# Tile-by-tile waits behind a closed pool, and three more steps at the entry of an interleaved attention

## The chip, the cores and the metric

The kernel runs on one core of one Trainium2 chip. Five engines work side by side, each through its own row of instructions in a fixed order, and wait for one another by semaphores: TensorE (PE in the profile), VectorE (DVE), ScalarE (ACT), GpSimd (POOL) and SyncE (SP), which issues most of the transfers (DMAs). The metric is the device time of one execution in microseconds (us).

## The reference, cut to what matters

Three stages follow one another: a masked attention over 4 batches, 8 heads, 576 positions and 64 columns; a dense layer that multiplies two projections; and a mixture of 8 experts of which each token uses the best two.

```python
scores = scale * np.matmul(q, k.transpose(0, 1, 3, 2))
mask_local = (rel >= 0) & (rel < 32)                       # heads 0 to 3
mask_strided = (rel >= 0) & (pos[None, :] % 32 == pos[:, None] % 32)   # heads 4 to 7
attn = softmax(np.where(masks, scores, -1e9))
x = (attn @ v).transpose(0, 2, 1, 3).reshape(2304, 512)

x = ((x @ w_a) * (x @ w_b)) @ w_out                        # 512 -> 1536 -> 512

noisy = x @ w_gate + np.log1p(np.exp(x @ w_noise)) * noise
top2 = np.argpartition(-noisy, 2, axis=1)[:, :2]           # weights: softmax of the two
out[mask] += top2_w * (np.maximum(x[mask] @ w1[e], 0.0) @ w2[e])
```

`w_a`, `w_b` and `w_out` arrive as 64-bit numbers.

## The kernel before, in words

**Arithmetic.** A product of 32-bit matrices is done as three matmuls on a high and a low part of each operand (`mm3`, L196 to L198). The weights of the dense layer are read as 64-bit words (`load_raw`, L168; tiles named `raw`) and taken apart on ACT (L178, L179, L182) and DVE (L177, L181, L184 to L186): that is "the conversion" of a block, done in two steps of a generator `conv`. A `raw` tile is one of three that are used in turn, so a load waits for the conversion three blocks earlier.

**Start.** A pool `setup` holds helper tiles from which DVE and POOL build the masks (L78 to L111; the last one is L90 on DVE). It is closed, and the pools `ring`, `stage` and `router` (L147 to L149) take over its memory. The first loads of q, k and v go into tiles of `ring` (named `qkv`, L229 to L244). Meanwhile PE runs 14 matmuls on ones (L75), which only occupy it.

**Attention.** A `Unit` is a pair of heads of one batch. Its work is cut into small methods: `T` transposes q and k (L258; copies L260, L262), `Q` computes scores of one half (L281, L290) and, after its second call, the softmax (`E`: L294, L296, L314 to L327 on DVE, L300, L318, L323 on ACT), `P` transposes probabilities (L335, copy L336), `PV` multiplies by v (L348, copy L351). `att_pipe` strings them into steps; each `yield` ends a step. For each unit the steps are Q(0,0), Q(0,1), then P(1,0) and P(1,1) of the unit before, Q(1,0), PV(1) of the unit before, Q(1,1), two T of the next unit, P(0,0), P(0,1), two T, PV(0). For the first unit of a pipe there is no unit before, and the three steps P, P and PV are left out altogether. A finished unit's tail columns go out by a store into `tails` (L353), issued by SP.

**Two pipes.** The four units of batch 0 run first, alone, with the first 12 conversion steps dealt out over their steps (`conv_to(min(12, i * 12 // 50))`, `i` counts the steps); PE's order there is the scheduler's, by its own model of the times. The twelve units of batches 1 to 3 are a second pipe, interleaved with the dense layer. This layer goes over five chunks of columns (`c`) and twelve blocks (`f`): `stage_a` computes `pa` and `pb` (12 matmuls each) and multiplies them (L703, L708 to L710), `stage_b` adds to `po` (12 matmuls). After each of these groups `point()` advances the second pipe by up to two steps. Here PE's order is the program's; DVE's and ACT's are the scheduler's. At the last block of a chunk, attention steps that the next chunk needs are run off in one go.

**Routing.** After a chunk, `finish` and `route` choose experts and write a table by eight indirect stores from POOL (L510) out of a tile `pay`, of which there are two. Its columns of token numbers are copied by DVE (L501); the scheduler places that copy early, for a `pay` that is used later, so it waits until the stores out of the tile two chunks earlier have landed. Then come the experts (`ph`, `py`), which the change does not touch.

**Small PSUM tiles.** All `tt` tiles (transposes, scores, PV of the second pipe) share two banks: a PE instruction that writes one waits until ACT or DVE has copied out the one before the last.

Of the kernel before, what the change touches and what calls it, by code (L numbers as in the profile page):

```python
# [32 lines left out]
def attention_moe_kernel(ctx: ExitStack, tc: tile.TileContext, q, k, v, w_a, w_b, w_out,  # L33
# [110 lines left out]
            yield  # L144


    ring = ctx.enter_context(tc.tile_pool(name="ring", bufs=1))  # L147
    stage = ctx.enter_context(tc.tile_pool(name="stage", bufs=1))
    rpool = ctx.enter_context(tc.tile_pool(name="router", bufs=1))  # L149

    def load_unit(src, hi, lo):

# [204 lines left out]
    def att_pipe(us, ahead, done, may=lambda u: True):  # L357

        for i in range(4):
            us[0].T(i)
            yield
        if ahead < len(us):
            us[ahead].load_qk()
        for n, u in enumerate(us):
            last = us[n - 1] if n else None
            nxt = us[n + 1] if n + 1 < len(us) else None
            for x in range(2):
                u.Q(0, x)  # L370
                yield
            if last:
                for x in range(2):
                    last.P(1, x)
                    yield
            u.Q(1, 0)
            yield
            if last:
                last.PV(1)
                done(last)  # L380
                if ahead == 1:
                    u.load_v()
                yield
            u.Q(1, 1)
            yield
            for i in range(2):
                if nxt:
                    nxt.T(i)
                    yield
            for x in range(2):  # L390
                u.P(0, x)
                yield
            for i in range(2, 4):
                if nxt:
                    nxt.T(i)
                    yield
            if nxt and n + 1 + ahead < len(us):
                us[n + 1 + ahead].load_qk()
            while not may(u):
                yield  # L400
            u.PV(0)
            yield
        for x in range(2):
            u.P(1, x)
            yield
        u.PV(1)
        done(u)
        yield
# [262 lines left out]
    with tc.manual_schedule(engines={mybir.EngineType.SP}):  # L671
        for i, u in enumerate(us):
            u.load_qk()
            u.load_v()
            conv_room["ahead"](min(i + 1, 3))
        later = [Unit(atile, bank1, b, hp, "act" if b == 1 else "dve", (b > 1,) * 2) for b in range(1, B) for hp in HPS]
        later[0].load_qk()
        later[0].load_v()
        for i, _ in enumerate(att_pipe(us, 9, lambda u: split_kd(0, u.hp))):
            conv_to(min(12, i * 12 // 50))  # L680
        conv_to(12)
        late_load()
# [4 lines left out]
    attended = set()  # L687
    may = [1]
    attq.append(att_pipe(us, 1, lambda u: attended.add((u.b, u.hp)), lambda u: u.b <= may[0]))

    def stage_a(c, f, point):
# [331 lines left out]
```

## Time and profile before

| | us |
|---|---|
| median of 3 runs | 1148.36 |
| their lowest and highest | 1148.26, 1151.85 |
| the profiled execution, its device time | 1152.77 |
| its span (first to last instruction) | 1150.9 |
| busy: PE | 1104.0 |
| busy: DVE, ACT, POOL | 511.5, 433.3, 142.8 |
| mean granted TensorE clock (1 is full speed) | 0.955 |

PE is counted busy for 96% of the span. So a gain must come from the few stretches where PE stands, or where its clock is granted at half. In the 40 slices of the page (28.8 us each) both lie at the front: the clock digits are 6, 5, 5 and 8 in the first four slices, and 9 (full) in nearly all others. Rows of the timeline give start and duration of an instruction, and in brackets how long its engine stood idle before it and what ended that.

### The profile page before, as it was taken

The numbers are of one execution on the slowest core, as the hardware profiler recorded it, in microseconds if no ns is written. First come the engines' busy times: TensorE is split into PE (matmuls) and PEld (weight loads), VectorE is DVE, ScalarE is ACT, GpSimd is POOL, SyncE is SP. The second block draws the span as 40 slices with busy tenths as digits, with TensorE's granted clock in tenths as the row PEclk, the third lists the DMA queues.
The fourth block names the chain that finished last, engine by engine and source line by source line (L and its number), as shares of the span: only waits on it lengthen the run. The fifth ranks groups of instructions, "written<-read, shape, count | busy, mean of one in ns | idle before, by whom it ended". The sixth has DMA issues, their size and how long they took to land.

```text
span 1150.9 us, 16118 instructions
## 1 busy us (share of the span) xinstructions
PE 1104.0 (96%) x6411; PEld 934.6 (81%) x6411; DVE 511.5 (44%) x1075; ACT 433.3 (38%) x935; POOL 142.8 (12%) x136
## 2 busy tenths in 40 slices
PE   7988999999999999999997999999999999999996
PEld 4756777787787877888887989998999899998995
DVE  4839787845446354223125452255343434342211
ACT  4757877533233232212124442244242323332110
POOL 0000000001000020002000314231021312121112
PEclk6558999999999999999999999999999999999998
DMA  8444443310112111730003443176344544442123
GB/s 168 112 132 135 141 146 105 78 59 12 36 36 63 39 17 49 267 118 1 1 37 94 132 142 55 42 176 178 111 113 126 121 117 118 120 111 47 19 29 48
DMA packets 88549, 105.02 MB, mean 91 GB/s; under 512 B 43664, under 2 KB 48400, under 8 KB 88464
## 3 DMA queue, kind: packets, MB, share of 16 engines
q1 hardware_dynamic: 78352, 82.89, 24.4%
q0 software_dynamic: 10112, 21.02, 10.0%
q8 instruction: 52, 0.85, 0.3%
q14 instruction: 33, 0.27, 0.1%
HBM read 78.53 MB, written 25.35 MB: 90 GB/s over the span
## 4 chain that ended last, share of the span: by engine, by line
PE 81%; DMA 6%; DVE 4%; ACT 4%; issue 2%; POOL 1%; SPq 1%; ACTq 0%; DVEq 0%; POOLq 0%
PE ph L197 6%; PE ph L196 6%; PE ph L198 6%; PE py L196 6%; PE py L197 6%; PE py L198 6%; PE po L196 4%; PE pa L196 4%; PE pb L196 4%; PE po L198 4%; PE po L197 4%; PE pb L197 4%; PE pb L198 4%; PE pa L197 4%; PE pa L198 4%; PE tt L290 2%
## 5 line engine op out<-in xcount | busy, mean ns | idle before, releaser
L873 DVE SCALAR_TENSOR_TENSOR hl<-ph,hh 128x256 fp32r<-128x256 f32 (+1 forms) x128 | 62.4, 489 | 214.4 <-ACT hh L872 213.8
L872 ACT ACTIVATE hh<-ph 128x256 fp32r<-128x256 f32 (+1 forms) x128 | 55.1, 433 | 226.3 <-PE ph L198 222.2
L708 DVE TENSOR_TENSOR a<-a,pb 128x512 f32<-128x512 f32 (+1 forms) x60 | 37.9, 631 | 128.2 <-PE pb L198 128.1
L897 POOL DMA_INDIRECT out_dram<-y,tb x40 | 64.5, 1612 | 185.3 <-ACT y L896 144.0
L510 POOL DMA_INDIRECT table<-pay,sli x36 | 35.8, 994 | 412.8 <-DVE sli L498 321.6
L703 ACT ACTIVATE a<-pa 128x512 f32<-128x512 f32 (+1 forms) x60 | 33.1, 551 | 127.6 <-PE pa L198 127.5
L709 ACT ACTIVATE gh<-a 128x512 fp32r<-128x512 f32 (+1 forms) x60 | 35.1, 586 | 79.2 <-DVE a L708 78.9
L763 POOL DMA_INDIRECT g<-x,tb x40 | 40.0, 1000 | 188.1 <-PE tt L772 166.1
L710 DVE TENSOR_TENSOR gl<-a,gh 128x512 fp32r<-128x512 f32 (+1 forms) x60 | 38.0, 634 | 17.7 <-ACT gh L709 17.3
L335 PE MATMUL tt<-ident,s 72*72 72x72 f32 (+1 forms) x224 | 30.7, 269 | 10.1 <-DVE sst L326 4.4
L290 PEld LDWEIGHTS tt<-kT,qT 64*72 64x72 f32 (+1 forms) x336 | 29.6, 149 | 11.9 <-issue 9.8
L335 PEld LDWEIGHTS tt<-ident,s 72*72 72x72 f32 (+1 forms) x224 | 23.2, 144 | 18.8 <-ACT a L703 4.8
L290 PE MATMUL tt<-kT,qT 64*72 64x72 f32 (+1 forms) x336 | 37.7, 254 | 0.0
L336 ACT ACTIVATE pT<-tt 128x288 f32<-128x288 f32 (+1 forms) x64 | 25.2, 407 | 30.9 <-PE tt L335 30.8
L196 PE MATMUL py<-w6h,hh 128*128 128x512 f32 x80 | 31.9, 401 | 2.8 <-ACT hh L872 2.8
L196 PE MATMUL pa<-xh,w0h 128*128 128x512 f32 (+1 forms) x80 | 32.7, 409 | 1.5 <-ACT xh L414 1.4
L196 PE MATMUL pb<-xh,w1h 128*128 128x512 f32 (+1 forms) x80 | 32.7, 409 | 0.0
L196 PE MATMUL py<-w2h,hh 128*128 128x512 f32 x80 | 31.9, 401 | 0.0
L196 PE MATMUL py<-w3h,hh 128*128 128x512 f32 x80 | 31.8, 398 | 0.0
L197 PE MATMUL py<-w6l,hh 128*128 128x512 f32 x80 | 31.8, 397 | 0.0
L196 PE MATMUL pa<-xh,w3h 128*128 128x512 f32 (+1 forms) x80 | 31.7, 396 | 0.0
L197 PE MATMUL py<-w3l,hh 128*128 128x512 f32 x80 | 31.6, 395 | 0.0
(294 smaller groups left out, 3294.9 us busy)
## 6 DMA issues: line engine op xcount, KB each, us to landing
st<-in_moe_w_dram SPq DMA_DIRECT2D x64, 512.0 KB
out_dram<-zero SPq DMA_DIRECT2D x13, 512.0 KB
raw<-in_moe_w_a_dram SPq DMA_DIRECT2D x4, 1024.0 KB
raw<-in_moe_w_b_dram SPq DMA_DIRECT2D x4, 1024.0 KB
raw<-in_moe_w_out_dram SPq DMA_DIRECT2D x4, 1024.0 KB
x<-row SPq DMA_DIRECT2D x16, 256.0 KB
raw<-in_moe_w_a_dram SPq DMA_DIRECT2D x4, 512.0 KB
raw<-in_moe_w_b_dram SPq DMA_DIRECT2D x4, 512.0 KB
```

Source lines behind the costliest of these rows:

```text
L196: nc.tensor.matmul(ps, w[0], x[0], start=start, stop=False)
L197: nc.tensor.matmul(ps, w[0], x[1], start=False, stop=False)
L198: nc.tensor.matmul(ps, w[1], x[0], start=False, stop=stop)
L290: nc.tensor.matmul(ps[:, ii, :], self.qT[r0:r0 + 64, q0:q0 + n], self.kT[r0:r0 + 64, k0:k0 + m], start=not pemask, stop=not pemask or ii = ...
L335: nc.tensor.transpose(ps[:, ii, :], self.s[half][:, x, ii, :], ident[:n, :n])
L510: ins = nc.gpsimd.indirect_dma_start(out=table, out_offset=bass.IndirectOffsetOnAxis(ap=sli[:, 2 * j + kk:2 * j + kk + 1], axis=0), in_=pa ...
L708: nc.vector.tensor_mul(a, a, pb)
L710: behind[0] = nc.vector.tensor_sub(gl, a, gh.bitcast(F32))
L763: nc.gpsimd.indirect_dma_start(out=g, out_offset=None, in_=x2, in_offset=bass.IndirectOffsetOnAxis(ap=TB[e, t][:, 0:1], axis=0))
L872: nc.scalar.activation(hh, ph, AF.Relu)
L873: nc.vector.scalar_tensor_tensor(hl, ph, 0.0, hh.bitcast(F32), op0=OP.max, op1=OP.subtract)
L897: ins = nc.gpsimd.indirect_dma_start(out=out, out_offset=bass.IndirectOffsetOnAxis(ap=TB[e, t][:, 0:1], axis=0), in_=y, in_offset=None, co ...
```

## The change

Three pools get `reuse_waits="tile"`: where such a pool takes memory that an earlier pool has given back, each of its tiles waits for the earlier tiles that it overlaps, and no longer for the whole earlier pool. And in `att_pipe` the three steps of the unit before are now yielded also where there is no unit before: they are empty steps of the first unit of a pipe, three for each of the two pipes.

```diff
-    ring = ctx.enter_context(tc.tile_pool(name="ring", bufs=1))
-    stage = ctx.enter_context(tc.tile_pool(name="stage", bufs=1))
-    rpool = ctx.enter_context(tc.tile_pool(name="router", bufs=1))
+    ring = ctx.enter_context(tc.tile_pool(name="ring", bufs=1, reuse_waits="tile"))
+    stage = ctx.enter_context(tc.tile_pool(name="stage", bufs=1, reuse_waits="tile"))
+    rpool = ctx.enter_context(tc.tile_pool(name="router", bufs=1, reuse_waits="tile"))
...
-            if last:
-                for x in range(2):
+            for x in range(2):
+                if last:
                     last.P(1, x)
-                    yield
+                yield
             u.Q(1, 0)
             yield
             if last:
...
                 if ahead == 1:
                     u.load_v()
-                yield
+            yield
             u.Q(1, 1)
```

The engines' rows change in many places, since the schedule is made anew, up to the second chunk of the dense layer; from there on they are almost the same.

The first place is SP's row at the start of the program, with the semaphores that an instruction waits for. Before:

```order
L229 DMA qkv_177<-in_q_dram 96x6x64 [waits DVE_49,Pool_49]
L229 DMA qkv_177<-in_q_dram 96x6x64
L229 DMA qkv_177<-in_k_dram 96x6x64 x2
L237 DMA qkv_182<-in_v_dram 128x2x64
L240 DMA qkv_182<-in_v_dram 128x5x64 x2
L168 DMA raw<-in_moe_w_a_dram 128x4x256
```

Now:

```order
L229 DMA qkv_177<-in_q_dram 96x6x64 x2
L229 DMA qkv_177<-in_k_dram 96x6x64 x2
L237 DMA qkv_182<-in_v_dram 128x2x64
L240 DMA qkv_182<-in_v_dram 128x5x64 x2
L168 DMA raw<-in_moe_w_a_dram 128x4x256
```

The first load, and with it all that stands behind it, no longer waits for DVE and POOL.

The second place is DVE's row where the second pipe starts inside the dense layer. `s_885` and `sst_886` are scores and sums of the first half of its first unit; those of the second half are `s_928` and `sst_929` before, `s_944` and `sst_945` now; `raw_861` is the first weight block of the following pair of `f`. Before:

```order
L314 TENSOR_REDUCE sst_929<-s_928 96x6
L185 TENSOR_SCALAR raw_663<-ct_265 128x1024
L710 TENSOR_TENSOR gl_924<-a_859,gh_923 128x512
L321 TENSOR_SCALAR sst_929<-sst_929 96x6
L181 SCALAR_TENSOR_TENSOR ct_265<-raw_796,ct_265 128x1024
L186 SCALAR_TENSOR_TENSOR w1l_157<-raw_663 128x4x256
L185 TENSOR_SCALAR raw_796<-ct_265 128x1024
L325 TENSOR_SCALAR sst_886<-sst_886 96x6
L186 SCALAR_TENSOR_TENSOR w2l_159<-raw_796 128x1024
L326 RECIPROCAL sst_886<-sst_886 96x6
L325 TENSOR_SCALAR sst_929<-sst_929 96x6
L327 TENSOR_TENSOR s_885<-s_885,sst_886 96x768
```

Now:

```order
L185 TENSOR_SCALAR raw_633<-ct_265 128x1024
L710 TENSOR_TENSOR gl_924<-a_859,gh_923 128x512
L186 SCALAR_TENSOR_TENSOR w1l_157<-raw_633 128x4x256
L181 SCALAR_TENSOR_TENSOR ct_265<-raw_796,ct_265 128x1024
L325 TENSOR_SCALAR sst_886<-sst_886 96x6
L177 TENSOR_SCALAR ct_265<-raw_861 128x1024
L185 TENSOR_SCALAR raw_796<-ct_265 128x1024
L326 RECIPROCAL sst_886<-sst_886 96x6
L314 TENSOR_REDUCE sst_945<-s_944 96x6
L186 SCALAR_TENSOR_TENSOR w2l_159<-raw_796 128x1024
L327 TENSOR_TENSOR s_885<-s_885,sst_886 96x768
```

The second half's sums no longer stand ahead of the first half's last step L327, but its reduction L314 still does, and the first conversion of `raw_861` (L177) has moved in ahead of it. On PE, four groups of 12 matmuls instead of three now lie between the scores of the first half and its transposes L335, which wait for L327.

The third place is DVE's row in the second chunk, at the early copy into `pay`. Before:

```order
L302 TENSOR_TENSOR s_2696<-tt_2730,maskAB_72 96x384
L314 TENSOR_REDUCE sst_2697<-s_2696 96x6
L501 COPY pay_4728<-ids_80 128x4 x2
L317 TENSOR_TENSOR s_2696<-s_2696,sst_2697 96x768
L319 TENSOR_REDUCE sst_2697<-s_2696 96x6
```

Now:

```order
L302 TENSOR_TENSOR s_2696<-tt_2730,maskAB_72 96x384
L314 TENSOR_REDUCE sst_2697<-s_2696 96x6
L317 TENSOR_TENSOR s_2696<-s_2696,sst_2697 96x768
L501 COPY pay_4728<-ids_80 128x4 x2
L319 TENSOR_REDUCE sst_2697<-s_2696 96x6
```

The subtraction L317, for which ACT's exponentials (L318) wait, has moved from behind the copy to ahead of it.

## Rows read from the trace of the kernel before

**Rows 1.** Page: granted clock in 40 slices of 28.8 us, in tenths.

```profile
PEclk6558999999999999999999999999999999999998
```

**Rows 2.** Windows: length, busy (x count) per engine, clock, DMA share, GB/s.

```profile
25.00:30.00 5.00, 5.00 (x42) 3.60 (x40) 3.97 (x8) 4.29 (x11) 0.00 (x0) 0.50 0.99 253
```

**Rows 3.** Waits of SP in 0 to 6 us: total, times, longest.

```profile
SPq L229 <- DVE maskAB L90: 4.4, 1, 4.4
```

**Rows 4.** Timeline of all engines, 0 to 45 us: start, duration, instruction, idle before.

```profile
1.07 6.01 PE L75 MATMUL idle<-ones 128*128 128x512 bf16 x14 [1.07 <-DVE ones L77]
...
5.21 1.41 SPq L229 DMA_DIRECT2D qkv<-in_q_dram  x2
...
9.30 0.69 PE L258 MATMUL sc<-ident,qkv 96*128 96x96 f32 x6 [2.22 <-DMA qkv<-in_q_dram]
...
22.05 0.65 ACT L179 ACTIVATE raw<-raw 128x512 uint32<-128x512 uint32 x1 [2.93 <-DMA raw<-in_moe_w_b_dram]
```

**Rows 5.** Timeline of ACT, 60 to 125 us.

```profile
72.73 1.10 ACT L179 ACTIVATE raw<-raw 128x1024 uint32<-128x1024 uint32 x1 [2.45 <-DMA raw<-in_moe_w_out_dram]
```

**Rows 6.** Chain of work that ended last, 55 to 80 us: start, duration, what.

```profile
55.82 5.19 DMA raw<-in_moe_w_a_dram
...
66.14 0.34 SPq L353
...
66.58 6.08 DMA raw<-in_moe_w_out_dram
...
76.61 0.80 PE pa L196
```

**Rows 7.** Timeline of DVE, 40 to 140 us, the end of batch 0.

```profile
56.36 0.69 DVE L415 TENSOR_TENSOR xl<-xf,xh 128x512 fp32r<-128x512 f32 x1 [0.46 <-ACT xh L414]
...
64.22 0.69 DVE L186 SCALAR_TENSOR_TENSOR w2l<-raw 128x512 fp32r<-128x512 uint32 x1
```

**Rows 8.** Windows of one us, as rows 2.

```profile
62.00:63.00 1.00, 0.46 (x3) 0.45 (x3) 1.00 (x2) 1.00 (x4) 0.00 (x0) 0.50 0.94 346
...
100.00:101.00 1.00, 0.30 (x2) 0.00 (x0) 1.00 (x2) 1.00 (x6) 0.00 (x0) 1.00 1.27 252
```

**Rows 9.** Timeline of PE at the entry of the second pipe.

```profile
97.26 0.48 PE L196 MATMUL pa<-xh,w0h 128*128 128x512 f32 x1
...
104.71 1.19 PE L335 MATMUL tt<-ident,s 96*128 96x96 f32 x6 [4.41 <-DVE sst L326]
```

**Rows 10.** Windows around the fall of the clock at the entry, as rows 2.

```profile
102.70:109.10 6.40, 4.39 (x14) 3.72 (x15) 4.98 (x9) 5.97 (x13) 0.00 (x0) 0.50 0.88 321
```

**Rows 11.** Timeline of DVE at the entry.

```profile
96.26 0.94 DVE L314 TENSOR_REDUCE sst<-s 96x6 f32<-96x768 f32 x1
...
98.93 1.23 DVE L181 SCALAR_TENSOR_TENSOR ct<-raw,ct 128x1024 int32<-128x1024 int32 x1 [0.45 <-ACT ct L178]
...
103.08 0.18 DVE L326 RECIPROCAL sst<-sst 96x6 f32<-96x6 f32 x1
...
103.62 0.95 DVE L327 TENSOR_TENSOR s<-s,sst 96x768 f32<-96x768 f32 x1
...
105.58 0.68 DVE L177 TENSOR_SCALAR ct<-raw 128x1024 int32<-128x1024 int32 x1
```

**Rows 12.** DVE's groups, 85 to 105 us: count, busy, mean ns, idle before.

```profile
L185 DVE TENSOR_SCALAR raw<-ct 128x1024 int32<-128x1024 int32 x3 | 2.0, 683 | 0.0
...
L186 DVE SCALAR_TENSOR_TENSOR w2l<-raw 128x1024 fp32r<-128x1024 uint32 x1 | 1.2, 1224 | 0.0
```

**Rows 13.** Timeline of SP: the load of the block that DVE needs next.

```profile
95.69 0.39 SPq L168 DMA_DIRECT2D raw<-in_moe_w_a_dram  x1
```

**Rows 14.** Timeline of DVE and ACT in the second chunk.

```profile
296.45 0.24 DVE L501 COPY pay<-ids 128x4 int32<-128x4 int32 x2 [4.70 <-DMA table<-pay,sli]
296.60 0.95 DVE L317 TENSOR_TENSOR s<-s,sst 96x768 f32<-96x768 f32 x1
297.58 0.84 ACT L318 ACTIVATE s<-s 96x768 f32<-96x768 f32 x1 [6.55 <-DVE s L317]
...
301.34 0.45 DVE L260 COPY kT<-tt 128x288 f32<-128x288 f32 x1
```

**Rows 15.** Timeline of PE there.

```profile
299.26 0.47 PE L335 MATMUL tt<-ident,s 96*128 96x96 f32 x3 [2.49 <-ACT qT L262]
```

**Rows 16.** Windows after it, as rows 2.

```profile
299.30:304.30 5.00, 5.00 (x20) 4.01 (x21) 3.08 (x7) 1.24 (x3) 0.00 (x0) 0.66 0.00 0
```

## The prediction

> **What bounds the kernel now.** I read the page's slices first. The granted clock stands at 5 to 6 tenths in the first three slices of 28.8 us and at 8 in the fourth, then near 9 almost throughout [rows 1]. A clock of 0.50 is 1.2 GHz, the lower of TensorE's two levels; 1.00 is 2.4 GHz. PE is busy for 96% of the span, so whatever keeps PE standing, or lets its clock fall, adds to the time almost one for one, and idle time of any other engine adds only where PE waits for it. I then read SP's waits and the timeline from the start for the first part of the change, and DVE's, ACT's and PE's timelines at the three places where the rows of the engines move. Four places come out.
>
> Start: SP's first load waits 4.4 us for the last DVE instruction of the masks [rows 3], is issued at 5.21, and PE, which has spent 1.07 to 7.08 on its 14 idle matmuls, stands 2.22 us for q [rows 4].
>
> End of batch 0: the last weight block is issued at 66.58, directly behind a tails store at 66.14, and takes 6.08 us; ACT stands 2.45 us for it, and PE's first dense matmuls come at 76.61 [rows 5, 6].
>
> Entry of the second pipe: PE stands 4.41 us for the first half's softmax, until 104.71 [rows 9], and the clock is at 0.50 for the 6.40 us around it, with 4.39 us of PE's work in them [rows 10].
>
> Second chunk: DVE's early copy into `pay` stands 4.70 us for the routing stores, with L317 behind it [rows 14]; PE stands 2.49 us [rows 15] and runs the next 5 us at a mean clock of 0.66 [rows 16].
>
> **The change part by part.**
>
> *A, tile waits at the start.* One wait of 4.4 us goes; SP then starts at about 0.8 (5.21 − 4.4). It goes wholly only if the chain behind it is one of transfers. PE alone could use just the 2.22 us that it waited, because its idle matmuls end at 7.08. But in the first phase attention and conversion share DVE, ACT and three raw tiles; at 22.05 ACT stands 2.93 us for the `w_b` block [rows 4], which shows that transfers were still behind there, and all of these start 4.4 us earlier. So the ends are 2.2 and 4.4, and I take 4.4. The masks are no new wait: the old wait ended when they were done, at 5.21, and PE's first scores come only after 9.30 [rows 4]. A gain of clock is excluded: the half clock lasts through this phase with PE counted busy 5.00 of 5 us [rows 2].
>
> *B, conversion three steps earlier in batch 0.* The last weight load now stands ahead of the last two tails stores in SP's row, and its raw tile comes free with a conversion that stands 6 instead of 16 DVE instructions behind L415; these are 56.36 and 64.22 before [rows 7], so it can be issued up to about 7 us earlier. Two loads stand in front of it (the first 55.82 to 61.01 [rows 6]), and the stretch 62 to 63 still moves 346 GB/s [rows 8], so I expect it to land at about 68 to 70 in the old scale instead of 72.66. That removes the 2.45 us in front of ACT, but ACT's L179 of 1.10 us [rows 5] now stands ahead of the last unit's copies of probabilities, so part of it moves onto the path. Ends: 2.45, and −1.1 if the early L179 costs its own length and nothing else comes. I take 1.5, nearer to the wait seen than to the cover lost. The rows on the two loads in front bear on this: the first was in use from 61.01 on, while bytes still moved at 346 GB/s between 62 and 63 [rows 6, 8], so loads came one after the other and not all at the end.
> The Trainium skill, page "DMA: Bandwidth & Descriptors", section "Issuing engines are not separate DMA queues", says the opposite: all transfers run on the same sixteen engines and interleave, whichever engine started them. By that rule a third load issued early slows the two in front, B is about 0, and the time 1137.6; the order of landing here speaks rather for the first reading.
>
> *C, the entry.* Before: 4.41 us of standing and, for 4.39 us of work at half clock, 2.2 us lost; together 6.6. Now one more group of 12 matmuls lies between the scores and the transposes. The group of 97.26 ended at 104.71 − 4.41 = 100.30 [rows 9], its next would begin about 0.2 earlier, so a group is worth 2.8 and PE is ready at about 103.1. The other side also moves. On DVE, L177 of the next block now stands ahead of L327, and that block's load is issued at 95.69 [rows 13]. The nearest load took 5.19 us [rows 6], which gives 100.9; 100 to 101 still moves 252 GB/s [rows 8]; I take 101.5. The copy of 105.58 before [rows 11] is the other bound, since by then it had certainly landed. From L177 on stand L177 (0.68), L185 (0.68), L326 (0.18), L314 (0.94), L186 (1.22) and L327 (0.95) [rows 11, 12]: 4.65 less about 0.08 of overlap at each of five seams, 4.25. So L327 ends at 105.75 and PE starts near 105.8: a wait of 2.7 instead of 4.41. The clock loss I take from the second chunk, where a wait of 2.49 was followed by 5 us at 0.66, that is 3.4 us at half, a loss of 1.7 [rows 15, 16]. Left over 4.4 of 6.6; C is 2.2. Ends: 6.6 if no wait is left, and −2.4 if the block lands as late as 105.58 (a wait of 6.8 and 2.2 of clock, 9.0 in all).
>
> *D, second chunk.* L317 now stands ahead of the waiting copy, so ACT's exponentials (0.84 us, before them 6.55 us of idle time) and the copies of q behind them no longer wait [rows 14]. The 2.49 of standing and 1.7 of clock go: 4.2. What is late next: the copy still holds L319, L327, L708 and L710, and then the copies of k (301.34 before [rows 14]). The copy ends at about 296.7, as before, and k's first copy then ended at 301.34 + 0.45 = 301.79, with L317 and the exponential (0.95 and 0.84) in between; these two go and L710 with ACT's part of it comes ahead of k, about as much, so k is copied by about 301.8 again. PE has, from 299.26 − 2.49 = 296.77 on [rows 15], two groups of 2.8 us and some four small bundles of transposes (0.47 the one shown, about 0.3 net of overlap) before it needs the tile, until about 303.5. Some 1.7 us of slack cover it; a table store that starts over 1.7 us later than now (relative to PE) would eat into the gain. Ends 0 and 4.2; I take 4.2.
>
> Everything behind the second chunk keeps its order and I count it at nothing; the cover is that PE's rows there are the same.
>
> Sum: 4.4 + 1.5 + 2.2 + 4.2 = 12.3. The profiled execution took 1152.77 (its span 1150.9), so it would be 1140.5; it lies 4.41 above the median of 1148.36, and taken off the median the sum gives **1136.1 us**. The four ends add up to −1.4 and 17.7, or 1149.8 and 1130.7.
>
> **The rivals.** A difference of 0.3%, 3.4 us, is about what the measurement can tell from none.
>
> 1. *The stores' wait only moves (D = 0).* The copy keeps its 4.70 us on DVE; if k's copies come late, PE stands there instead. For: everything behind L317 still waits. Against: the slack above. 1140.3.
> 2. *DVE or the load becomes the bound at the entry (C = −2.4).* For: L177 before was first started at 105.58 and nothing shows an earlier landing; DVE stood only 0.45 us in this stretch before L181 [rows 11]. Against: the bytes end near 101. 1140.7.
> 3. *The entry's wait vanishes (C = 6.6).* The three empty steps cover it if the block lands before 98.5. Against: bytes still move at 100. 1131.7.
> 4. *The start does only half of what it says (A = 2.2).* PE's idle matmuls stay where they are and the first units are bound by PE at half clock: for it speaks PE busy 5.00 of 5 [rows 2]. 1138.3.
> 5. *Two of A, C and D fail together.* For instance D = 0 and C = −2.4 leave 3.5 of the 12.3 and the median less about 3: no change that can be told.
> 6. *Slower: the clock stays down after the entry.* PE's waits of 103 us and later follow one another more closely, the clock is not raised, and all of PE's work runs at 1.2 GHz meanwhile. Each us so costs 0.5. To lose 3.4 against before it must first eat the 12.3, so it decides from about 31 us of low clock on, to beyond 137; the price is then 1152 or more. For: the clock stayed at 0.50 in the first phase with a PE counted as busy throughout [rows 2]. Against: after 104.71 it was back within 4.4 us [rows 10].
>
> The Trainium skill, page "TensorE: Matmul & The Clock Gate", section "HAM oscillation — how this bites in real kernels", says that a wait in the middle of a loop lets the clock fall and the burst behind it then starts cold, each time. Both falls here follow a wait, as it says; by that rule alone rival 6 would need wait after wait, which the change gives no row for.
>
> **How the numbers follow.** My forecast, all four terms near their values, 0.42, with a range of its own of 1133 to 1139; rival 1, 0.15; rival 2, 0.14; rival 3, 0.10; rival 4, 0.07; rival 5, 0.07; rival 6, 0.05. The range from 1131 to 1143 takes in the forecast and rivals 1 to 4, and leaves out rivals 5 and 6 and some of the tails, under 2 in 10. Faster: all but rivals 5 and 6, 0.88; the same 0.07; slower 0.05.
>
> **What would show it.** A: SP's first load at about 0.8 and ACT's `w_b` conversion at about 17.7; wrong if PE starts q's transposes earlier but the dense layer does not. B: the first dense matmuls at about 70.7 (76.61 − 5.9); above 72.2 B is not there. C: PE's wait in front of the first L335 of the second pipe at 2.7 and a shorter stretch at 0.50; wrong if it is 4.4 or more. D: no standing of PE in the second chunk around 287, and L501 waiting behind L317; wrong if a wait of PE of some 2 us for k or its like stands there. The whole is wrong above 1143, or if the gain lies at a fifth place.

## The result and the profile after

The changed kernel took 1138.08 us (median of 4 executions, 1137.87 to 1142.42), the kernel before in the same comparison 1150.11: a ratio of 0.9897 with a 95% interval of 0.9874 to 0.9920, or 9 to 14 us less. Repeated in a later comparison, the ratio was 0.9918 (0.9892 to 0.9945). The forecast was 1136.1, with a range from 1131 to 1143. The profiled execution took 1142.42 us with a span of 1140.6, where before had 1152.77 and 1150.9.

The granted clock in 40 slices of the changed kernel, against [rows 1]: the first, third and fourth slice have gained one or two tenths, and two later slices, at about 600 to 627 and 770 to 798 us, have lost one.

```profile
PEclk7579999999999999999998999998999999999998
```

**Start.** The timeline of all engines of the changed kernel, 0 to 30 us (start, duration, instruction, idle before). It answers to [rows 4]; SP's wait of [rows 3] is gone.

```profile
0.76 1.41 SPq L229 DMA_DIRECT2D qkv<-in_q_dram  x2
1.07 4.70 PE L75 MATMUL idle<-ones 128*128 128x512 bf16 x14 [1.07 <-DVE ones L77]
...
5.62 0.66 PE L258 MATMUL sc<-ident,qkv 96*128 96x96 f32 x6
...
19.21 0.65 ACT L179 ACTIVATE raw<-raw 128x512 uint32<-128x512 uint32 x1 [4.17 <-DMA raw<-in_moe_w_b_dram]
```

The first load is issued 4.45 us earlier (0.76 for 5.21), and PE begins without a wait. The `w_b` block, which I had expected at 17.7, comes at 19.21: only 2.84 earlier. Windows of the changed kernel (length, busy of PE, PEld, DVE, ACT and POOL, clock, DMA share, GB/s) show why part may be lost on the way:

```profile
14.00:18.00 4.00, 2.78 (x18) 2.07 (x16) 1.68 (x5) 1.04 (x6) 0.00 (x0) 0.55 1.02 176
18.00:22.00 4.00, 0.76 (x5) 0.62 (x6) 0.04 (x1) 2.79 (x14) 0.00 (x0) 0.50 1.20 176
```

The DMA engines are full (share 1.02 and 1.20) while PE is busy for 0.76 of 4 us: this stretch is bound by transfers, as assumed, and how fast they run (176 GB/s here) sets how much of the earlier issue arrives.

**End of batch 0.** First a load from the chain of waits, then ACT's timeline and PE's; they answer to [rows 5, 6].

```profile
57.17 6.55 DMA raw<-in_moe_w_out_dram
```

```profile
63.81 1.14 ACT L179 ACTIVATE raw<-raw 128x1024 uint32<-128x1024 uint32 x1 [0.92 <-DMA raw<-in_moe_w_out_dram]
```

```profile
70.69 0.80 PE L196 MATMUL pa<-xh,w0h 128*128 128x512 f32 x1 [1.44 <-ACT xh L414]
```

The block is converted 8.9 us earlier than before (63.81 for 72.73); ACT's wait is 0.92 instead of 2.45. The dense layer starts at 70.69, 5.92 us earlier; the forecast said 70.7.

**Entry of the second pipe.** DVE's timeline and PE's, against [rows 9, 11]:

```profile
94.87 0.69 DVE L177 TENSOR_SCALAR ct<-raw 128x1024 int32<-128x1024 int32 x1 [0.96 <-DMA raw<-in_moe_w_a_dram]
...
96.19 0.91 DVE L314 TENSOR_REDUCE sst<-s 96x6 f32<-96x768 f32 x1
...
98.15 0.95 DVE L327 TENSOR_TENSOR s<-s,sst 96x768 f32<-96x768 f32 x1
```

```profile
99.24 0.44 PE L335 MATMUL tt<-ident,s 96*128 96x96 f32 x3 [2.06 <-DVE s L327]
```

And the windows around the fall of the clock, against [rows 10]:

```profile
97.00:100.00 3.00, 0.94 (x8) 0.76 (x7) 3.00 (x4) 2.54 (x4) 0.00 (x0) 0.96 0.45 110
100.00:103.00 3.00, 3.00 (x9) 2.33 (x8) 3.00 (x6) 2.26 (x11) 0.00 (x0) 0.50 1.00 348
```

DVE does wait for the block's load (0.96), as the working had it, and L327 ends at 99.10. PE stands 2.06 us (forecast 2.7, before 4.41), and about 3 us at half clock follow, where before 4.39 us of work ran at it.

**Second chunk.** DVE's timeline, against [rows 14]:

```profile
284.61 0.95 DVE L317 TENSOR_TENSOR s<-s,sst 96x768 f32<-96x768 f32 x1
285.49 0.23 DVE L501 COPY pay<-ids 128x4 int32<-128x4 int32 x2
286.48 0.95 DVE L319 TENSOR_REDUCE sst<-s 96x6 f32<-96x768 f32 x1 [0.76 <-ACT s L318]
```

All waits of PE from 85 to 400 us (total, times, longest) are now these two; the one of [rows 15] is not among them:

```profile
PE tt L335 <- DVE s L327: 2.1, 1, 2.1
PE tt L290 <- ACT pT L336: 1.1, 1, 1.1
```

But the copy did not wait at all here, so this profile does not show that its new place mattered. DVE itself was late: it added the masks (L302) only at 283.04, though PE's scores for it were done at 280.19, and the profile names no engine of this core for what it waited for ("remote"):

```profile
283.04 0.55 DVE L302 TENSOR_TENSOR s<-tt,maskAB 96x384 f32<-96x384 f32 x1 [6.09 <-remote]
```

Matched group by group, the dense layer of the two profiles is 10 us apart ahead of this place and about 14 behind the fourth chunk. At the end only 10.3 are left. One place where something was given back is the first expert; ACT and PE there:

```profile
769.23 1.15 ACT L159 ACTIVATE w3h<-st 128x512 fp32r<-128x512 f32 x2 [5.00 <-DMA st<-in_moe_w_dram]
```

```profile
770.71 0.79 PE L196 MATMUL py<-w6h,hh 128*128 128x512 f32 x1 [4.01 <-ACT hh L872]
```

ACT's copy that PE needs is queued behind the conversion of an expert's block, which waits for its load. The kernel before had 2.8 us of this wait at 780.94. That was not foreseen. Another place is the last chunk: from the routing of the fourth chunk to that of the fifth the changed kernel took 61.7 us (616.18 to 677.89), the kernel before 59.4 (629.94 to 689.33).

### The profile page after: what moved, and what is told of

Read it like the earlier page. It is cut to its first block, busy times and chain, and to the rows that moved or that the text cites. A ratio compares the mean times of both kernels' runs of the same rounds, so it can differ in the third digit from the quotient of the medians.

```text
span 1140.6 us, 16116 instructions
## 1 busy us (share of the span) xinstructions
PE 1097.2 (96%) x6411; PEld 929.8 (82%) x6411; DVE 511.5 (45%) x1075; ACT 432.3 (38%) x935; POOL 141.8 (12%) x136
## 3 DMA queue, kind: packets, MB, share of 16 engines
q0 software_dynamic: 10112, 21.02, 10.2%
## 4 chain that ended last, share of the span: by engine, by line
PE 81%; DVE 7%; DMA 6%; ACT 3%; issue 1%; another core or an unknown queue 1%; SPq 1%; POOL 0%; ACTq 0%; POOLq 0%; DVEq 0%
PE ph L196 6%; PE ph L198 6%; PE ph L197 6%; PE py L196 6%; PE py L197 6%; PE py L198 6%; PE pa L196 4%; PE pb L196 4%; PE po L196 4%; PE pb L197 4%; PE pb L198 4%; PE pa L197 4%; PE pa L198 4%; PE po L198 4%; PE po L197 4%; PE tt L290 2%
## 5 line engine op out<-in xcount | busy, mean ns | idle before, releaser
L709 ACT ACTIVATE gh<-a 128x512 fp32r<-128x512 f32 (+1 forms) x60 | 35.1, 586 | 70.7 <-DVE a L708 57.2
L290 PEld LDWEIGHTS tt<-kT,qT 64*72 64x72 f32 (+1 forms) x336 | 29.5, 149 | 13.4 <-issue 10.3
L335 PE MATMUL tt<-ident,s 72*72 72x72 f32 (+1 forms) x224 | 29.4, 263 | 4.2 <-DVE s L327 2.1
L335 PEld LDWEIGHTS tt<-ident,s 72*72 72x72 f32 (+1 forms) x224 | 22.3, 140 | 12.6 <-ACT qT L262 2.9
L196 PE MATMUL pb<-xh,w4h 128*128 128x512 f32 (+1 forms) x80 | 31.5, 394 | 0.6 <-issue 0.6
```

The lines of the kernel that those rows point to most:

```text
L196: nc.tensor.matmul(ps, w[0], x[0], start=start, stop=False)
L290: nc.tensor.matmul(ps[:, ii, :], self.qT[r0:r0 + 64, q0:q0 + n], self.kT[r0:r0 + 64, k0:k0 + m], start=not pemask, stop=not pemask or ii = ...
L335: nc.tensor.transpose(ps[:, ii, :], self.s[half][:, x, ii, :], ident[:n, :n])
```

## The experiments

Each ratio is that to runs of the kernel before in the same comparison (median 1150.13 for experiments 1 to 4, 1150.03 for 6 to 8, 1154.50 for 9 to 12), so that ratios can be set side by side and times cannot. The kernels take the change apart, then vary it.

**1. The tile waits alone.**

```diff
-    ring = ctx.enter_context(tc.tile_pool(name="ring", bufs=1))
+    ring = ctx.enter_context(tc.tile_pool(name="ring", bufs=1, reuse_waits="tile"))
```

and so for `stage` and `router`. 

> Only the three pools' tile waits, without the empty steps; every engine's row is as before, only SP's first load waits for nothing. My theory: the first phase is a chain of transfers and conversions, so the whole 4.4 us arrive: first dense matmuls of the last kd at 72.2 instead of 76.61, the total 4.4 less than before, the stands of PE at the entry (4.4) and in the second chunk (2.5) still there. Rival (PE or ACT at half clock bounds the first units): only about 2 to 3 us arrive, dense layer at 73.5 to 74.4.

Measured: 0.9967 (0.9953 to 0.9981), 3.8 us less. The dense layer starts at 73.56, that is 3.05 earlier in these two profiles; this lay with the rival. Of the second chunk the theory was wrong. PE there, and DVE:

```profile
294.64 0.47 PE L335 MATMUL tt<-ident,s 96*128 96x96 f32 x3 [0.82 <-ACT qT L262]
```

```profile
291.83 0.24 DVE L501 COPY pay<-ids 128x4 int32<-128x4 int32 x2 [0.64 <-DMA table<-pay,sli]
```

DVE's order is as in the kernel before, with L317 behind the copy, but the copy waits 0.64 and not 4.70, and PE stands 0.82 and not 2.49.

**2. The empty steps alone**, with the pools as before. 

> Only the empty steps, the pools wait as before; the rows of DVE, ACT and SP are those of the changed kernel. My theory: without the 4.4 us of the start, the rest (1.5 at the end of batch 0, about 4.3 at the entry and 4.4 in the second chunk, and a wait of 1.9 in the third chunk) makes 8 to 12 us; the first load is at 5.2, the dense layer starts at about 75.1. Rival (the terms are not independent: an earlier start is what lets the block at the entry land in time): PE's wait at the entry grows beyond the 2.06 us of the changed kernel.

Measured: 0.9959 (0.9941 to 0.9978), 4.7 us less, under the 8 to 12 expected. The dense layer starts at 73.47, so the steps of the first pipe are worth as much as the tile waits. PE's wait at the entry is 2.2 as in the changed kernel: the rival, that the entry needs the earlier start, falls.

**3. Tile waits, and the steps only in the first pipe.**

```diff
-                yield
+                if last or ahead == 9:
+                    yield
```

(`ahead` is 9 in the first pipe and 1 in the second; so at both places.) 

> Tile waits, and the empty steps only in batch 0's pipe. My theory: start and end of batch 0 as in the changed kernel (dense layer at 70.7), 5.9 us less than before in all; the entry (PE stands 4.4) and the second chunk (2.5) as before, since DVE's order there is as before. Rival: the second chunk's stand goes too, because it depended on when the chunk starts and not on the order of L317 and the copy; then about 10 us less.

Measured: 0.9939 (0.9920 to 0.9957), 7.0 us less. The dense layer starts at 70.78 and PE stands 4.4 at the entry, as expected. The second chunk is the surprise again; PE and DVE (the copy's line is two further down in this kernel):

```profile
291.38 0.47 PE L335 MATMUL tt<-ident,s 96*128 96x96 f32 x3 [0.37 <-ACT qT L262]
```

```profile
288.57 0.24 DVE L503 COPY pay<-ids 128x4 int32<-128x4 int32 x2 [0.19 <-DMA table<-pay,sli]
```

**4. The kernel before with five `pay` tiles.**

```diff
-        pay = rpool.tile([128, J, 2, 2], I32, name="pay", tag="pay", bufs=2)
+        pay = rpool.tile([128, J, 2, 2], I32, name="pay", tag="pay", bufs=5)
```

> The kernel before with five tiles for pay instead of two, so that the early copies into pay wait for no store; nothing else of the change. My theory: PE's 2.49 us of standing in the second chunk and the fall of the clock behind it go, 4.2 us, and the 1.89 us in the third chunk too: 5 to 6 us less than before. Rival: something else holds PE there (the q copies or the exponentials come late for another reason): PE stands as before and nothing is gained.

Measured: 1.0011 (0.9994 to 1.0028): no gain. In its profile PE has no stand left at that place. The further copies, free to run at once, went to the front of DVE's row ahead of the masks, and SP's first load was issued at 5.64 instead of 5.21. So the expected 5 to 6 us were not there in the time. The profile does not say that the place is worth nothing, though: from the fourth chunk's routing to the end it took 523.8 us, where the kernel before took 521.0 and, in a second profile, 521.4.

**5. The kernel before once more, for a second profile.** 

> The kernel before once more, for a second profiled execution. My theory now: the landing of the routing stores differs from one execution to the next, and the first profile of the kernel before was a late one; here DVE's copy into pay waits 0.2 to 1.5 us instead of 4.70, PE stands under 1 us in the second chunk instead of 2.49, the wait in the third chunk is under 3 instead of 6.07, and the execution is 3 to 5 us shorter than 1152.77. Rival (the stand belongs to the order of L317 behind the copy, and the kernels with tile waits or more pay tiles escaped it by their timing): the waits are 4.7 and 2.5 again.

Measured: 1152.95 us in its one execution. First DVE at this place in the first profile of this kernel, then DVE, PE and the windows behind it in the second:

```profile
290.22 0.55 DVE L302 TENSOR_TENSOR s<-tt,maskAB 96x384 f32<-96x384 f32 x1 [3.08 <-PE tt L290]
```

```profile
294.91 0.55 DVE L302 TENSOR_TENSOR s<-tt,maskAB 96x384 f32<-96x384 f32 x1 [5.47 <-remote]
```

```profile
298.31 0.24 DVE L501 COPY pay<-ids 128x4 int32<-128x4 int32 x2 [1.87 <-DMA table<-pay,sli]
```

```profile
301.12 0.47 PE L335 MATMUL tt<-ident,s 96*128 96x96 f32 x3 [2.05 <-ACT qT L262]
```

```profile
301.00:306.00 5.00, 4.88 (x37) 4.08 (x38) 3.69 (x8) 1.76 (x5) 0.00 (x0) 1.00 0.00 0
```

Between the two: the copy waited 1.87, PE stood 2.05, but the clock did not fall. The place costs 4.2 in one execution of this kernel, 2.05 in another, 0.8 and 0.4 in the two kernels that have its order there (experiments 1 and 3). The last of the eight stores is issued at 290.23 in the first profile and has landed 6.2 us later; in the second these are 292.52 and 5.8, with the tile waits alone 287.31 and 4.5, and in experiment 3 284.51 and at most 4.1. PE's stands, 2.49, 2.05, 0.82 and 0.37, go with these landings. The copy's wait does not: it fell by 2.83 between the two profiles of one program, the landing by 0.4. The rest is DVE, which came to the copy 1.5 us behind the last store's issue in the first profile and 3.9 in the second, where L302 began at 294.91 though PE's scores were done at 292.48; what held it there stays open. My expectation of under 1 us of standing and a shorter execution failed, and so did the rival's 2.5 with a copy wait of 4.7. The start differed as well: the same program began its dense layer at 79.03, 2.4 us later than in the first profile.

**6. The changed kernel once more.** 

> The changed kernel once more, for a second profile and a tighter ratio. If its parts are 3.0 (tile waits), 2.8 (steps in the first pipe) and 2.5 to 4.3 (steps in the second pipe): 8.5 to 10 us less than before, ratio 0.9915 to 0.9925. By the forecast with its fourth term: 12 us less, 0.9895.

Measured: 0.9918 (0.9892 to 0.9945), median 1139.9. By itself it sides with the smaller sum, but the interval reaches 0.9895 too, and the first comparison gave that. The dense layer starts at 69.47, PE waits 2.0 at the entry, nothing in the second chunk, and 4.3 at the first expert.

**7. Tile waits, and the steps only in the second pipe** (`ahead == 1` in the diff of experiment 3). 

> Tile waits, and the empty steps only in the second pipe. My theory: start 3.0 and entry 2.8 us (net of work that only moves behind the first chunk), together about 6 less than before, and the first dense matmuls at about 73.5; the entry's wait near 2. Rival (the entry needs the conversion that the first pipe's steps have brought forward): PE's wait at the entry stays above 3.5 and the total is under 5.

Measured: 0.9950 (0.9933 to 0.9968), 5.7 us less. The dense layer starts at 73.01, PE waits 2.1 at the entry. As expected; the rival falls.

**8. Three more steps.**

```diff
+            for _ in range(3 if ahead == 1 and not last else 0):
+                yield
             u.Q(1, 0)
```

> The changed kernel with three further empty steps ahead of the second pipe's P, so six there. My theory: the entry's stand of 2.06 us goes and with it the fall of the clock behind it (1.7 of loss), since another group of 12 matmuls or two cover it; the steps that are run off at the end of the first chunk become about five and cost under 1 us: 2 to 4 us less than the changed kernel. Rival (DVE or the block's load falls further behind whatever PE does, so the stand only moves): no change, and a stand of about 2 at the next instruction that waits for DVE.

Measured: 0.9995 (0.9977 to 1.0012): the whole gain of the change is gone, and neither theory had this. The stand of 2.06 is not there, but these are (waits of PE from 80 to 215 us), and then the windows at the end of the first chunk:

```profile
PE pb L198 <- DVE w4l L186: 3.2, 1, 3.2
PE tt L335 <- ACT qT L262: 2.5, 2, 1.5
PE tt L290 <- ACT xf L351: 2.0, 1, 2.0
...
```

```profile
203.00:210.00 7.00, 4.96 (x38) 3.85 (x38) 5.28 (x11) 3.01 (x6) 0.26 (x1) 0.74 0.12 29
210.00:217.00 7.00, 7.00 (x38) 5.40 (x35) 4.45 (x11) 2.66 (x5) 0.00 (x0) 0.78 0.33 82
```

DVE, which converts for the dense layer, comes late in another place, and the steps run off at the end of the chunk have no matmuls of the dense layer between them: PE stands 2.0 of 7 us and the clock is low in part of both windows. Summed over the first chunk, from the dense layer's start to the routing, PE stood 8.4 us and lost 9.8 to the low clock, against 3.4 and 4.2 in the changed kernel. These 10.6 us are about the gain that is gone.

**9 to 11. Two, one and four steps in the second pipe,** with the tile waits and three steps in the first, in one comparison. The yields there are left out, or added ahead of Q(1,0):

```diff
-                yield
+                if last or ahead == 9 or x < 1:
+                    yield
...
-            yield
+            if last or ahead == 9:
+                yield
```

is one step; with `x < 2` it is two. 

> Tile waits, three empty steps in the first pipe, two instead of three in the second. Four groups of matmuls still lie ahead of the first transposes, L317 stands ahead of the pay copy, and no step has to be run off at the end of the first chunk. My theory (the entry is decided by the groups in front of it): PE's wait at the entry about 2 as in the changed kernel, no stand in the second chunk, total within 2 us of the changed kernel, rather better. Rival (each empty step counts): wait near 3, total 1 to 3 us worse than the changed kernel.

> Tile waits, three empty steps in the first pipe, one in the second. The first transposes come at the same place of PE's row as without empty steps, but L317 stands ahead of the pay copy. This parts the fourth term from the third: my theory says that PE's wait at the entry is 4 or more again and the stand in the second chunk is gone, so the total lies 0 to 2 us below the kernel with steps in the first pipe only (0.9939 of before). Rival (the fourth term is a large one also in usual executions): 4 us below it.

> Tile waits, three empty steps in the first pipe, four in the second. My theory: the entry's wait falls under 1.5, because a fifth group lies ahead of the transposes, but the steps run off at the end of the first chunk grow to three and PE waits there for ACT and DVE: 0 to 4 us slower than the changed kernel. Rival (more room is simply better): 1 to 3 us faster than the changed kernel.

Measured: two steps 0.9920 (0.9894 to 0.9946), one step 0.9891 (0.9862 to 0.9920), four 0.9882 (0.9853 to 0.9911). The intervals overlap, and that of the changed kernel's 0.9897 with all of them; no order among them is shown. With two steps the entry's wait fell to 0.51, not 2 as I had said, and two others came behind it:

```profile
121.73 0.76 PE L258 MATMUL tt<-ident,ql 96*128 96x96 f32 x6 [2.15 <-ACT xf L351]
...
134.47 1.23 PE L348 MATMUL tt<-pT,vl 72*64 72x72 f32 x16 [2.11 <-ACT kT L262]
```

With one step the entry's wait is 3.67, a little under the 4 expected. What it was run for shows in DVE's row:

```profile
285.30 0.24 DVE L503 COPY pay<-ids 128x4 int32<-128x4 int32 x2 [3.64 <-DMA table<-pay,sli]
```

The copy waits 3.64 us, and PE has no stand of even 0.2 us between 270 and 300. With two and four steps it waits 3.20 and 3.63, also without a stand of PE there. The ratio with one step lies 0.0048 below that of experiment 3, measured in another comparison; the rival's 4 us can't be excluded from that. With four steps PE does not wait at the entry, as expected, but 0.8, 1.2 and 1.0 us at 166, 177 and 208 us; the 0 to 4 us of loss that were expected from the end of the chunk do not show in the time. So the entry's wait went from 3.67 to nothing over these kernels, and the time did not follow it.

**12. The changed kernel with five `pay` tiles** (the diff of experiment 4). 

> The changed kernel with five tiles for pay. With tile waits the further copies ahead of the masks no longer delay the first load. My theory: no wait for the stores is left in the second and third chunk, PE did not stand there in most executions, so the total is the changed kernel's to within 1.5 us. Rival (the copy's wait costs PE time by other paths): 2 to 4 us faster than the changed kernel.

Measured: 0.9876 (0.9849 to 0.9903), the lowest ratio of all, but its interval holds the changed kernel's 0.9897. In its profile neither the second nor the third chunk holds a wait of PE for the copies of k; in the three other kernels of the same comparison, with two `pay` tiles, there are 2.0 to 2.3 us of it in the third chunk, in the changed kernel's own two profiles 0.6 at most. It would be the version to keep, if one had to choose; that it is faster than the changed kernel is not shown.

## Why the prediction was right, and what in it was not

The time, the sign and the four places came out. The sum of 12.3 stood against a measured 11.8 in the first comparison and 9.4 in the second, by the ratios. But three of its four terms had other sizes, B and C larger and D mostly smaller, a part counted at nothing took about 3 us back, and the errors cancelled. That the total came within 1 us in the first comparison is in part luck. That the dense layer began at 70.69 where 70.7 was forecast was luck as well, as the profiles of all kernels together show. The start of the dense layer (the first `pa` matmul behind the last `xh`), grouped by what a kernel has of the change in the first phase:

| first phase | starts in its profiles, us | mean |
|---|---|---|
| as before | 76.61, 79.03 | 77.8 |
| tile waits only | 73.56, 73.01 | 73.3 |
| steps only | 73.47 | 73.5 |
| both | 70.69, 69.47, 70.78, 70.43, 69.30, 68.37, 70.42, 70.03 | 69.9 |

(Experiment 4, whose first load comes 0.43 later than before, starts at 78.62.) Profiles of the same order differ by 2.4 us here, so one pair can't size a term of 1.5.

**A, 4.4 forecast: about 4.** 77.8 to 73.3 is 4.5, 73.5 to 69.9 is 3.6; the time of the whole kernel moved by 3.8 (2.2 to 5.4). The reading that transfers bound the phase, and not PE, fits best: between the groups no two profiles are closer than 2.7, though the interval of the time just reaches the other bound of 2.2. That the whole of it arrives was too exact. In the changed kernel the second block came 2.84 us earlier for a load queue started 4.45 earlier, with the DMA engines full.

**B, 1.5 forecast: about 3.4 to 4.3.** 73.3 to 69.9 and 77.8 to 73.5; by the total times it is 3.2 (experiment 3 less experiment 1). It was under-sized by taking the early L179 as moved onto the path. PE's wait for the last unit's probabilities, which this ACT instruction had held up, is 2.65 in the kernel with tile waits alone and under 0.2 at that place with the steps; the block's conversion now lies where PE has other units to work on. The price set against this, B near 0 because a third load slows the two in front, did not come: the third took 6.55 for 6.08 before, ACT stood only 0.37 us for the second, at 60.52, and the term did not shrink.

**C, 2.2 forecast: about 3.** The mechanism was right in each link (block load, L177, L327, PE). The block was there at 94.87, that is 100.8 with the dense layer's earlier start taken off, for the 101.5 assumed, and the wait was 2.06 for 2.7. To size C and D, the two chunks can be split. Each runs from the first `pa` of the table above, or from the routing's first matmul of the chunk in front (L485, or L487 in experiments 3 and 7), to its own routing. In windows of 2 us I add up PE's standing and what its busy time loses to the low clock; the rest is work at full clock.

| profile | chunk 1: stood and lost | rest | chunk 2: stood and lost | rest |
|---|---|---|---|---|
| before, first and second | 10.7, 10.5 | 191.1, 191.2 | 4.2, 2.1 | 135.2, 135.2 |
| experiments 1 and 3 | 10.8, 10.5 | 191.2, 191.5 | 0.8, 0.4 | 135.3, 135.3 |
| changed, first and second | 7.5, 7.9 | 190.0, 189.9 | 0.1, 0.1 | 136.6, 136.7 |
| experiments 2 and 7 | 7.5, 7.7 | 190.0, 189.9 | 0.1, 0.1 | 136.6, 136.7 |

The four without steps in the second pipe stand and lose 10.6 in the first chunk in the mean, the four with three steps 7.7: C is 2.9. (With one, two and four steps it is 9.3, 9.8 and 7.2, in one profile each.) They also do 1.3 us less work there, but 1.4 more in the second chunk: this is work that moved and no gain. By the total times the second pipe's steps, with D in them, are worth 1.9 (experiment 7 less experiment 1) to 4.8 (the first comparison less experiment 3).

**D, 4.2 forecast: 4.2 in that one profile, 0.4 to 2.1 in three others.** This step failed in size. The wait behind L317 is real: where L317 stands behind the copy, PE stood 2.49, 2.05, 0.82 and 0.37 in four profiles, and where it stands ahead, 0 to 0.2, even with a copy that waited 3.64. But its length goes with the landing of that execution's stores (6.2, 5.8, 4.5 and at most 4.1 us), and the fall of the clock of [rows 16] came with the longest of the four stands alone. The profiled execution lay 4.41 above the median, and I had taken the sum off the median without asking where the profile's excess sat. Up to 2.1 of it sat here, by the second profile: in the very term that I took from the first.

**Behind the second chunk, forecast at nothing.** This failed too: from the fourth chunk's routing to the end the two profiles of before took 521.0 and 521.4 us, the two of the changed kernel 524.4 and 524.5, so 3.0 to 3.5 us were given back. Some 1.2 to 1.9 of them are the first expert's wait (4.01 and 4.25 for 2.80 and 2.37), where the block's load landed 10.2 us earlier (769.23 for 779.47) while PE came 11.4 earlier; 0.9 to 2.3 lie in the last chunk. Coming early is not enough to cause it: with four steps, and in experiment 3, PE comes to this place as early, waits 2.43 and 2.37, and the part takes 520.8. But with the steps alone and in experiment 12 it takes 524.5 and 525.3. The cause stays open.

Of the rivals, "the wait only moves" is not borne out for D: with one, two and four steps the copy waits 3.2 to 3.64 and PE does not stand. The load did not become the bound at the entry, nor did the wait vanish there. The slower one, a clock that stays low after the entry, needed some 31 us; there were 3. Experiment 8 shows, though, that the side it stood for was near: three steps more and the gain was gone, by waits for DVE and the steps run off at the end of the chunk, which my forecast had not priced at all.

Two slips of the working change nothing: the lower ends add up to −1.3 (not −1.4), and for no wait at the entry the block would have had to land by 98.8 (not 98.5).

What stays open: how the 0.4% among the versions with one to four steps is ordered, how large D is in the mean, and what lengthens the part behind the fourth chunk. The first two would need more executions.

## What to carry to other kernels

Before a term is sized from one profile, look whether that execution lies above the median, and ask which of the waits in it end on a transfer; such a wait can differ from one execution to the next (4.70 and 1.87 us here), and a second profile of the same program is the cheapest way to see it. An order in which the instruction that others wait for stands ahead of one that waits on a transfer is worth having for the late landings alone. Splitting a stretch into standing, loss to the low clock and work, as in the table on C, parts a gain from work that only moved. And slack dealt into an interleaving can be paid back at its next fixed end: with one to four empty steps at the entry the gain stayed, with six it was gone.

## What the hardware showed that was not expected

- The landing of the last of eight small indirect stores behind its issue took 6.2 and 5.8 us in two executions of one program, and 4.5 and at most 4.1 at the same place of two others (experiments 1 and 3).
- The same program reached the end of its transfer-bound first phase at 76.61 and at 79.03 us, with the same first issue at 5.21.
- A stand of PE of 2.05 us was followed by no fall of the clock (1.00 in the 5 us behind it, second profile of the kernel before), one of 2.06 by some 3 us at 0.50 (entry of the changed kernel). The length of the stand alone did not decide it.
- DVE began an instruction at 294.91 whose input PE had finished at 292.48 (second profile of the kernel before), and one at 283.04 for 280.19 (changed kernel); in the first profile it began at 290.22, 0.04 us behind PE. The profile names nothing on this core for the 2.4 and 2.9 us.
